# Key products that read q from SBUF instead of PSUM in the first five items of a decode kernel's second attention

## The chip, the cores and the metric

The kernel runs on one core of a Trainium2 chip. The metric is device time in microseconds (us), the median of several executions; three executions of the kernel before took 2686.34 to 2686.61 us. Beside them stands one profiled execution, whose records are read below. Its engines are named as in the profile: PE (TensorE), DVE (VectorE), ACT (ScalarE), POOL (GpSimd) and SP (SyncE, which here issues the DMA transfers). SBUF is the memory that all engines work in, PSUM the one that PE writes to; POOL's operands all lie in SBUF in this kernel.

## The reference

Two layers, each an attention block over a long cache followed by a gated feed-forward block, for one new token of a batch of two; the same weights and caches serve both layers.

```python
def _A_ref(x, k_cache, v_cache, wq, wo):           # B=2, H=32, Sk=8192, Dh=128
    q = (x @ wq).reshape(B, Sq, H, Dh).transpose(0, 2, 1, 3)
    scores = jnp.einsum("bhqd,bhkd->bhqk", q, k_cache) * (Dh ** -0.5)
    p = _softmax(scores, axis=-1)
    o = jnp.einsum("bhqk,bhkd->bhqd", p, v_cache)
    return o.transpose(0, 2, 1, 3).reshape(B, Sq, H * Dh) @ wo

x = A_x
x = x + _A_ref(_layernorm(x), A_k_cache, A_v_cache, A_wq, A_wo)
x = x + _B_ref(_layernorm(x), B_w_gate, B_w_up, B_w_down)
x = x + _A_ref(_layernorm(x), A_k_cache, A_v_cache, A_wq, A_wo)
x = x + _B_ref(_layernorm(x), B_w_gate, B_w_up, B_w_down)
```

`_B_ref` is a GEGLU block of width 4608. Everything is float32. Keys and values of one layer are 2 x 2 x 32 x 8192 x 128 x 4 bytes, 537 MB, and nearly all of that is read once for each layer.

## The kernel before

**Items.** Attention is cut into 34 items. Items 0 to 29 hold two heads of one batch row each, items 30 to 33 one head. The 8192 keys of a head are spread over the partitions: an item of two heads gives every partition 128 keys, in eight parts of 16 keys (`JC`) by 128 numbers; an item of one head has 64 keys a partition, in four parts. The first attention goes through the items from 0 to 33, the second from 33 down to 0, so that some keys and values of the last items can stay in SBUF from the first attention to the second. The first five items of the second attention are 33, 32, 31, 30 (four parts each) and 29 (eight parts); for these `waited(n)` holds and every part is worked on by itself.

**Transfers.** All large transfers are issued by SP in one fixed order, planned ahead, into places of a big SBUF tile `space`. A transfer is issued when its place has been given back by the work that last read it: keys by the sums of a part (`add_up`, L671), values by the value products on PE (L800). If that work is late, so is the issue, and all that stand behind it on SP.

**One part of keys in the first five items of the second attention** (`multiply` and `add_up`):
- PE has made q of the item on all partitions, in one of two 128-column pieces of the PSUM tile `bank` (`query`, L599), one item ahead.
- ACT copies it to SBUF, `qs[:, n % 2, :]`, once an item (L650).
- DVE multiplies the first 12 of the 16 keys of each partition by q in PSUM (L651, 1536 numbers a partition).
- POOL multiplies the other 4 keys by q in `qs` (L655, 512 numbers), and then adds the right half of the first 9 keys' products to the left half (L668, 576 numbers; both inputs in `space`).
- ACT sums up each of the last 7 keys' products (L661), and DVE reduces the folded first 9 (L671) when the next part's product has been issued.

In the first and the last part of item 33 (`at_once`) POOL folds nothing, and DVE reduces 11 keys directly. After item 33's last product `qsb` gets its second half of the q sums (L933, DVE), from which the q of later items is made. At the end of an item come the maximum (L695 to L705), the exponentials (L728, ACT) and the value products (L800, PE). In all other items DVE does the whole product and POOL all the folding; there `weigh` (L766, L771) also weights some of the values on DVE with weights that it puts in PSUM (`share`), which POOL then adds up (L774).

Each engine works through its own instructions in the order of the program; waits between engines are by semaphores. The order is written by hand (`manual_schedule`) in the loop of `attention`: product of a part, then the sums of the part before.

Of the kernel before, what the change touches and what calls it, by code (L numbers as in the profile page):

```python
# [11 lines left out]
ALU = mybir.AluOpType  # L12
# [3 lines left out]
P = 128  # L16
# [3 lines left out]
DH = 128  # L20
# [4 lines left out]
JC = 16  # L25
# [98 lines left out]
def decode_layers(ctx, tc, x_in, kc, vc, wq, wo, wg, wu, wd, out):  # L124
# [423 lines left out]
    def attention(layer):  # L548
# [37 lines left out]
        qb, S, prod, rs, mT, tot, rinv, osb = {}, {}, {}, {}, {}, {}, {}, {}  # L586
# [17 lines left out]
        def waited(n):  # L604

            return layer == 1 and n in seq[:5]

        def at_once(n, k):

            return layer == 1 and n == seq[0] and k in (0, ITEMS[n].parts - 1)  # L610
# [13 lines left out]
        def own_rows(n, k, m):  # L624

            return 11 if at_once(n, k) else 9 if waited(n) else m * JC

        def keys(n, k, m):

            key = name("k", layer, n)  # L630
            if m == 1:
                return ready[key][k]
            return part_at(arena.live[key, k][0], m * PART).rearrange("p (j d) -> p j d", d=DH)
# [3 lines left out]
        def multiply(n, k, m):  # L637

            if k == 0:
                S[n] = work.tile([P, SK * 2 // P], F32, name="S")  # L640
            u = t = keys(n, k, m)
            if n == SINGLE[1] and k == 3 and layer == 0:
                nc.scalar.copy(kept, t)
            if layer == 0 and n in KEYS_HELD:
                u = ready["products"][k % 2]
            every = m * JC
            rows = 12 if waited(n) else every
            q = qs[:, n % 2, :]
            if rows < JC and k == 0:
                nc.scalar.copy(q, qb[n])  # L650
            nc.vector.tensor_tensor(  # L651
                out=u[:, :rows, :], in0=t[:, :rows, :], in1=qb[n].unsqueeze(1).to_broadcast([P, rows, DH]), op=ALU.mult
            )
            if rows < JC:
                nc.gpsimd.tensor_tensor(  # L655
                    out=u[:, rows:, :], in0=t[:, rows:, :], in1=q.unsqueeze(1).to_broadcast([P, JC - rows, DH]),
                    op=ALU.mult,
                )
            r = own_rows(n, k, m)
            for j in range(r, every):  # L660
                nc.scalar.activation(  # L661
                    u[:, j, :], u[:, j, :], AF.Copy, accum_out=S[n][:, k * JC + j:k * JC + j + 1]
                )
            if at_once(n, k):
                prod[n, k] = u[:, :r, :]
                return
            half = prod[n, k] = u[:, :r, :DH // 2]
            nc.gpsimd.tensor_tensor(out=half, in0=half, in1=u[:, :r, DH // 2:], op=ALU.add)  # L668
# [202 lines left out]
        for i, n in enumerate(seq):  # L871
# [18 lines left out]
            if first:  # L890
                highest(p)
                softmax(p)
            for j, (k, m) in enumerate(us):
                multiply(n, k, m)
                if j == 0 and not last and not first:
                    query(seq[i + 1])
# [37 lines left out]
        n, p = seq[-1], seq[-2]  # L934
# [154 lines left out]
```

## Time and profile before

| | us |
|---|---|
| median of three executions | 2686.34 |
| the profiled execution | 2686.49 |
| its span on the core | 2684.7 |
| second attention, first five items | about 1383 to 1464 of the span |

| engine | busy, us | share of the span |
|---|---|---|
| PE | 916.5 | 34% |
| DVE | 2028.0 | 76% |
| ACT | 163.8 | 6% |
| POOL | 1551.4 | 58% |

1154.23 MB moved in the span, on average 430 GB/s. A row of the timeline reads: start in us, duration in us, engine, line of the kernel, operation, what is written<-what is read, shapes, count, and in brackets the engine's idle time before it with what ended it. Where a row stands for several instructions, the duration covers them all. A row of the windows reads: stretch, its length, then the busy time and number of instructions of each engine, PE's granted clock, the busy share of the DMA engines and GB/s. A row of SP's waits reads: who waited<-for what: us in total, times, the longest. The slices are 40 equal parts of the span, 67.1 us each.

### The profile page before, as it was taken

What the parts mean: (1) busy time and instruction counts of PE and PEld (TensorE: products, weight loads), DVE (VectorE), ACT (ScalarE), POOL (GpSimd) and SP (SyncE); (2) the same over time, 40 slices, a digit from 0 to 9 for tenths busy, and PEclk for the clock granted to TensorE, in tenths of its full rate; (3) what the DMA queues carried; (4) which work ended last, traced back from release to release, by engine and by line L of the source; (5) the groups of instructions that cost most, each with busy time, mean ns of one, the idle gap of its engine ahead of it and who ended that gap; (6) DMA issues with size and microseconds to landing.
All of it is one profiled execution on the core that took longest, in us unless ns stands there. A gap on an engine that the chain in (4) does not pass through costs nothing. (4 is left out here: it accounts for less than half of the span.)

```text
span 2684.7 us, 16125 instructions
## 1 busy us (share of the span) xinstructions
PE 916.5 (34%) x6478; PEld 290.0 (11%) x6478; DVE 2028.0 (76%) x973; ACT 163.8 (6%) x786; POOL 1551.4 (58%) x405
## 2 busy tenths in 40 slices
PE   1323332232233233334563333223323323332355
PEld 0100000000001000111221101001000100010022
DVE  4878888888888888867038878888888888888740
ACT  0000000000000000000026000000000000000000
POOL 2546676667666766744028457666766676676520
PEclk7666655665566566566986665566566556655668
DMA  9999999999999999999999999999999999999998
GB/s 422 436 436 425 437 434 434 431 432 435 433 433 432 436 431 433 435 427 426 418 413 434 433 431 436 434 432 431 435 435 431 435 432 433 433 436 429 432 424 375
DMA packets 33947, 1154.23 MB, mean 430 GB/s; under 512 B 4152, under 2 KB 4176, under 8 KB 5968
## 3 DMA queue, kind: packets, MB, share of 16 engines
q1 hardware_dynamic: 33832, 1153.19, 99.8%
q8 instruction: 51, 0.84, 0.1%
q14 instruction: 24, 0.20, 0.0%
q10 hardware_dynamic: 40, 0.01, 0.0%
HBM read 1153.18 MB, written 0.00 MB: 430 GB/s over the span
## 5 line engine op out<-in xcount | busy, mean ns | idle before, releaser
L668 POOL TENSOR_TENSOR space<-space 128x3072 f32<-128x3072 f32 (+3 forms) x221 | 1128.1, 5104 | 487.7 <-DVE space L651 349.8
L651 DVE TENSOR_TENSOR space<-space,bank 128x6144 f32<-128x6144 f32 (+3 forms) x223 | 1112.7, 4990 | 312.9 <-DMA space<-in_A_k_cache_dram 249.6
L671 DVE TENSOR_REDUCE S<-space 128x48 f32<-128x3072 f32 (+3 forms) x223 | 569.3, 2553 | 89.4 <-POOL space L668 89.1
L774 POOL TENSOR_TENSOR space<-space 128x2048 f32<-128x2048 f32 x144 | 390.1, 2709 | 385.6 <-DVE space L771 370.2
L800 PE MATMUL acc<-space,prz 128*8 128x512 f32 x3328 | 510.1, 776 | 201.7 <-DMA space<-in_A_v_cache_dram 197.7
L599 PE MATMUL bank<-qsb,pick 4*64 4x128 f32 (+1 forms) x256 | 46.3, 436 | 857.2 <-DVE space L651 847.1
L771 DVE TENSOR_TENSOR space<-space,bank 128x4096 f32<-128x4096 f32 x48 | 212.2, 4420 | 1.6
L800 PEld LDWEIGHTS acc<-space,prz 128*8 128x8 f32 x3328 | 99.6, 107 | 553.9 <-issue 345.1
L720 ACT ACTIVATE nbs<-bank 128x2 f32<-128x2 f32 (+1 forms) x68 | 11.6, 171 | 1846.2 <-PE bank L705 1799.8
L822 PE MATMUL bank<-of,osb 128*32 128x2 f32 x512 | 40.9, 202 | 237.9 <-DVE osb L815 237.9
L599 PEld LDWEIGHTS bank<-qsb,pick 4*64 4x64 f32 (+1 forms) x256 | 20.6, 200 | 878.7 <-DVE space L651 859.3
L697 PE MATMUL bank<-ident,m 128*1 128x128 f32 x68 | 21.5, 317 | 246.2 <-DVE m L695 246.1
L524 POOL TENSOR_TENSOR rstd<-ve,mhalf 128x1 f32<-128x1 f32 x4 | 2.2, 550 | 168.8 <-DVE ve L522 168.8
L779 PE MATMUL acc<-space,owner 128*8 128x512 f32 x96 | 89.9, 1039 | 0.0
L1020 DVE STREAM_TRANSPOSE o<-o 128x288 f32<-128x288 f32 x4 | 2.8, 689 | 92.4 <-ACT o L1018 92.4
L822 PEld LDWEIGHTS bank<-of,osb 128*32 128x32 f32 x512 | 35.8, 154 | 326.2 <-DVE osb L815 324.9
L736 PE MATMUL bank<-sums,unit 128*128 128x2 f32 x120 | 35.3, 363 | 87.0 <-ACT prz L728 87.0
L814 DVE TENSOR_TENSOR acc<-acc,diag 128x512 f32<-128x512 f32 x64 | 43.5, 679 | 22.9 <-PE acc L800 22.9
L841 ACT ACTIVATE oT<-bank,rinv 32x8 f32<-32x8 f32 x110 | 28.6, 260 | 381.4 <-PE bank L822 380.8
L728 ACT ACTIVATE prz<-S,nbs 64x128 f32<-64x128 f32 (+1 forms) x128 | 50.7, 396 | 17.3 <-POOL prz L718 14.4
L528 DVE TENSOR_TENSOR x<-bank,x 128x144 f32<-128x144 f32 x4 | 1.2, 308 | 65.3 <-PE bank L1046 42.6
L661 ACT ACTIVATE space<-space 128x128 f32<-128x128 f32 x164 | 48.3, 296 | 23.6 <-DVE space L651 21.5
(80 smaller groups left out, 551.5 us busy)
## 6 DMA issues: line engine op xcount, KB each, us to landing
space<-in_A_v_cache_dram SPq DMA_DIRECT2D x8, 4096.0 KB
space<-in_A_k_cache_dram SPq DMA_DIRECT2D x6, 4096.0 KB
space<-in_A_wo_dram SPq DMA_DIRECT2D x15, 1152.0 KB
space<-in_A_k_cache_dram SPq DMA_DIRECT2D x15, 1024.0 KB
space<-in_B_w_down_dram SPq DMA_DIRECT2D x9, 1152.0 KB
space<-in_B_w_gate_dram SPq DMA_DIRECT2D x3, 3456.0 KB
space<-in_A_v_cache_dram SPq DMA_DIRECT2D x10, 1024.0 KB
space<-in_A_wq_dram SPq DMA_DIRECT2D x3, 3072.0 KB
```

The costliest lines, as they stand in the source:

```text
L599: nc.tensor.matmul(qb[n][to, :], pick[32 * c:32 * c + 4, r:r + 1].to_broadcast([4, P // it.heads]), qsb[32 * c:32 * c + 4, (h % 4) * DH:(h ...
L651: nc.vector.tensor_tensor(out=u[:, :rows, :], in0=t[:, :rows, :], in1=qb[n].unsqueeze(1).to_broadcast([P, rows, DH]), op=ALU.mult)
L661: nc.scalar.activation(u[:, j, :], u[:, j, :], AF.Copy, accum_out=S[n][:, k * JC + j:k * JC + j + 1])
L668: nc.gpsimd.tensor_tensor(out=half, in0=half, in1=u[:, :r, DH // 2:], op=ALU.add)
L671: nc.vector.tensor_reduce(out=S[n][:, k * JC:k * JC + own_rows(n, k, m)], in_=prod.pop((n, k)), axis=AX.X, op=ALU.add)
L728: nc.scalar.activation(pr[at, lo:].rearrange("p (g e) -> p g e", e=4)[:, 0:it.rows // 2:2, :], s[at, :it.rows].rearrange("p (g r) -> p g r ...
L771: nc.vector.tensor_tensor(out=t, in0=t, in1=share.unsqueeze(2).to_broadcast([P, rows, DH]), op=ALU.mult)
L774: nc.gpsimd.tensor_tensor(out=t[:, :rows], in0=t[:, :rows], in1=t[:, rows:2 * rows], op=ALU.add)
L779: nc.tensor.matmul(accumulator(n)[0:8, :], owner.rearrange("p a e -> p (a e)"), part_at(arena.live[key, lo][0], 4 * DH), start=False, stop ...
L800: nc.tensor.matmul(accumulator(n)[32 * c:32 * c + 8, :], pr[:, at:at + 8], t[g // 4][:, g % 4 * 4:g % 4 * 4 + 4, :].rearrange("p j d -> p ...
L814: nc.vector.tensor_tensor(out=q, in0=q, in1=diag.unsqueeze(2).to_broadcast([P, 4, DH]), op=ALU.mult)
L822: nc.tensor.matmul(po[lo:lo + 32, i, :], t[:, i::GH], of, start=True, stop=True)
```

## The change

In `multiply`, where the product on DVE is split with POOL (only in the first five items of the second attention), all parts behind an item's first read q from the SBUF copy `qs` that POOL reads already. An item's first part, and all products elsewhere, read PSUM as before.

```diff
             q = qs[:, n % 2, :]
             if rows < JC and k == 0:
                 nc.scalar.copy(q, qb[n])
+            by = q if rows < JC and k else qb[n]
             nc.vector.tensor_tensor(
-                out=u[:, :rows, :], in0=t[:, :rows, :], in1=qb[n].unsqueeze(1).to_broadcast([P, rows, DH]), op=ALU.mult
+                out=u[:, :rows, :], in0=t[:, :rows, :], in1=by.unsqueeze(1).to_broadcast([P, rows, DH]), op=ALU.mult
             )
```

`rows` is 12 in these items and `JC` 16; `k` is the number of the part. In the built program 19 of DVE's instructions name `qs` in place of `bank`; no instruction is added or moved on any engine. Of the waits, three products (the second parts of items 33, 31 and 30) lose one for PE, and the instruction of L933 gains one.

## The prediction

> **What bounds the kernel now.** I read the page first (shares, then the slices), then the windows of the changed stretch, SP's waits in it, and the instructions in order of time.
>
> ```profile
> span 2684.7 us, 16125 instructions
> ...
> PE 916.5 (34%) x6478; PEld 290.0 (11%) x6478; DVE 2028.0 (76%) x973; ACT 163.8 (6%) x786; POOL 1551.4 (58%) x405
> ...
> DMA  9999999999999999999999999999999999999998
> GB/s 422 436 436 425 437 434 434 431 432 435 433 433 432 436 431 433 435 427 426 418 413 434 433 431 436 434 432 431 435 435 431 435 432 433 433 436 429 432 424 375
> ```
>
> No engine is full; the DMA engines are, in nearly every slice, at about 433 GB/s. The time is the bytes over that rate, and an edit to the products can only move the end if it lets the transfers run dry, or ends a time when they did. The profiled execution took 2686.49 us, 1.79 more than its span and 0.15 more than the median 2686.34; the sum is made against 2686.49.
>
> The edit touches items 33, 32, 31, 30 (one head, four parts) and 29 (two heads, eight parts). These windows are items 32, 31, 30 and 29, each from its first product on DVE to the next item's (29 to POOL's last add):
>
> ```profile
> core 0: us, PE busy (x) PEld busy (x) DVE busy (x) ACT busy (x) POOL busy (x), PEclk, DMA share, GB/s
> 1403.32:1414.48 11.16, 5.95 (x34) 1.18 (x26) 8.98 (x8) 8.72 (x57) 10.48 (x8) 0.65 1.01 418
> 1414.48:1427.65 13.17, 7.73 (x35) 2.62 (x39) 10.12 (x11) 10.81 (x61) 10.59 (x8) 0.50 1.01 420
> 1427.65:1441.56 13.91, 7.55 (x41) 2.17 (x37) 11.25 (x14) 9.15 (x60) 10.48 (x8) 0.62 1.04 439
> 1441.56:1463.66 22.10, 8.90 (x61) 2.79 (x53) 21.47 (x21) 17.94 (x115) 20.95 (x16) 0.73 1.01 433
> ```
>
> DMA stays full here too (share 1.01 to 1.04), but POOL is nearly full as well: its idle time is 0.68, 2.58, 3.43 and 1.15 us, 7.8 in all, of 60.3. And the transfers hang on this work: SP's waits between 1384 and 1470 us are
>
> ```profile
> SPq L166 <- DVE S L671: 35.6, 9, 12.8
> SPq L166 <- PE acc L800: 31.1, 8, 9.7
> ```
>
> The next cache rows are issued when the sums of a part (L671) or the value products (L800) give their place back. Compute that is late here makes issues late; what shields the time is only how far the queue is ahead.
>
> **The change part by part.** 19 of the 24 products in this stretch (three in each of items 33 to 30, seven in item 29) get q from `qs`, in SBUF, in place of `bank`, in PSUM. No instruction is added, removed or reordered.
>
> *The wait.* Item 33's second product no longer waits for PE:
>
> ```profile
> 1382.98 1.75 DVE L651 TENSOR_TENSOR space<-space,bank 128x1536 f32<-128x1536 f32 x1 [11.02 <-ACT qs L650]
> 1384.77 1.62 DVE L671 TENSOR_REDUCE S<-space 128x11 f32<-128x1408 f32 x1
> 1391.94 3.42 DVE L651 TENSOR_TENSOR space<-space,bank 128x1536 f32<-128x1536 f32 x2 [5.56 <-PE bank L599]
> ...
> 1397.82 0.75 DVE L671 TENSOR_REDUCE S<-space 128x9 f32<-128x576 f32 x1
> 1398.49 0.74 DVE L933 SCALAR_TENSOR_TENSOR qsb<-acc,rstd,qsb 128x512 f32<-128x512 f32 x1
> 1399.15 1.61 DVE L671 TENSOR_REDUCE S<-space 128x11 f32<-128x1408 f32 x1
> ```
>
> PE's q products of item 32 stood behind the wq products in PE's queue. Now the two products can start at 1386.4, 5.5 us earlier; the wait for PE passes to L933, which came 6.5 us behind it and has cover. So item 33's work alone would end 5.5 us sooner. The second parts of items 31 and 30 lose the same wait, before which DVE was not idle.
>
> *The product by itself.* 1536 elements take 1.75 us with q in PSUM; the reduce L671 takes 1.62 for 1408 elements that all come from SBUF. Both are 1.14 to 1.15 ns an element, so I price the other memory at nothing.
>
> *The price of a second SBUF stream.* This is the term that decides. Until now a product takes one tensor from SBUF and q from PSUM, and POOL works beside it undisturbed. Item 29, once it runs evenly:
>
> ```profile
> 1450.64 1.27 POOL L655 TENSOR_TENSOR space<-space,qs 128x512 f32<-128x512 f32 x1
> 1451.87 1.42 POOL L668 TENSOR_TENSOR space<-space 128x576 f32<-128x576 f32 x1
> ...
> 1461.03 1.26 POOL L655 TENSOR_TENSOR space<-space,qs 128x512 f32<-128x512 f32 x1
> ```
> ```profile
> 1452.16 1.75 DVE L651 TENSOR_TENSOR space<-space,bank 128x1536 f32<-128x1536 f32 x1
> 1453.82 0.75 DVE L671 TENSOR_REDUCE S<-space 128x9 f32<-128x576 f32 x1
> 1454.48 1.74 DVE L651 TENSOR_TENSOR space<-space,bank 128x1536 f32<-128x1536 f32 x1
> ```
>
> POOL sets the pace: (1461.03 - 1450.64) / 4 = 2.60 us a part (four parts lie between the two L655 rows), back to back, with DVE's 1.75 + 0.75 beside it. Does a DVE instruction with both tensors in SBUF also run beside POOL? The only one near POOL's work is this:
>
> ```profile
> L766 DVE TENSOR_TENSOR bank<-prz x48: 199/201/201, 212.1 to 2497.2; 128x32 f32<-128x32 f32 x48
> ...
> 1604.07 0.20 DVE L766 TENSOR_TENSOR bank<-prz 128x32 f32<-128x32 f32 x1 [0.45 <-PE bank L697]
> ...
> 1608.86 4.50 POOL L774 TENSOR_TENSOR space<-space 128x2048 f32<-128x2048 f32 x1 [7.88 <-DVE space L771]
> ```
>
> It is short and falls into POOL's 7.88 us of idle time before L774, so the trace shows no meeting of the two, and the price has two ends. Low end: products still run beside POOL, pace 2.60, nothing added. High end: product and POOL's two instructions take turns, pace 2.60 + 1.74 = 4.34. The nearest row with two SBUF tensors is POOL's own: 1.42 us for 576 elements is 2.5 ns each, over twice DVE's 1.14 with the operands in two memories. A DVE product at twice its time, 3.48 + 0.75, would set a pace of about 4.2, close to the high end by another way. I take the high end.
>
> The Trainium skill speaks for the high end: its page "SBUF — State Buffer", section "Who interferes with whom", has a DVE instruction with two SBUF inputs contend with a GpSimd instruction that reads SBUF, through a shared read interface. The page's section "A bandwidth-pool intuition that's wrong (but worth ruling out)" lets a blocked side go on about 115 ns after the other's end; with that in place of the hand-over below, the sum would be 2 us higher. No row here can confirm either.
>
> *How late the stretch ends.* In items 32 to 29 16 products are changed: 16 x 1.74 = 27.8 us, if none of them falls into POOL's idle time; 20.0 if all of that 7.8 us is used. I take it that most can't be, since it lies at the head of an item (here of item 30), where both engines wait for ACT's copy of q and then for a first product that still reads PSUM:
>
> ```profile
> 1427.70 1.27 POOL L655 TENSOR_TENSOR space<-space,qs 128x512 f32<-128x512 f32 x1 [0.99 <-ACT qs L650]
> ```
>
> Item 33 taking turns: two products to 1389.8, then POOL's four instructions (1.41, 1.27, 1.41, 1.27, about 5.2 with their overlaps) to 1395.0, the third product to 1396.7, and the 2.94 us from 1397.82 to the end of the last reduce: 1399.7 in place of 1400.8, so 1.1 us is left of the 5.5. Each turn may cost a hand-over; POOL begins 0.09 us after the product it waits for (1391.94 + 1.75 against 1393.78 in the row below), so at most 0.09 x 2 x 16 = 2.9; I take half, 1.5.
>
> ```profile
> 1393.78 1.41 POOL L668 TENSOR_TENSOR space<-space 128x576 f32<-128x576 f32 x1 [8.25 <-DVE space L651]
> ```
>
> Item 29 ends late by 24 (between 20.0 - 1.1 = 19 and 27.8 - 1.1 + 2.9 = 29.6; 24 + 1.5 with hand-overs = 25.5).
>
> *What the queue covers.* An item's keys or values are 8.39 MB (two heads x 8192 x 128 x 4 bytes), 19.4 us at 433 GB/s; a half 9.7.
>
> ```profile
> 1432.90 10.39 SPq L166 DMA_DIRECT2D space<-in_A_k_cache_dram  x2
> 1447.26 6.72 SPq L166 DMA_DIRECT2D space<-in_A_v_cache_dram  x2
> 1466.91 0.33 SPq L166 DMA_DIRECT2D space<-in_A_k_cache_dram  x1
> 1488.50 0.33 SPq L166 DMA_DIRECT2D space<-in_A_v_cache_dram  x1
> ...
> 1499.99 34.44 DMA space<-in_A_k_cache_dram
> ```
>
> The keys issued at 1499.99 land at 1534.4 (the chain that ended last), so they begin at 1515.0; the values before them at 1495.6, the keys of 1467.2 at 1476.2: that issue is 9.0 us ahead. The two halves of values before it begin at 1466.5 and 1456.8, the second half of keys (issued by 1443.3) at 1447.1, 3.8 ahead, and the DMA share stays over 1; so a transfer needs less than 3.8 us from issue to its first byte. I take 2, and 7 us of cover at 1467.2 (between 5.2 and 9). At 1443.3 only 1.8 is covered against the delay of two to three items of three changed products (5.2 us each, less 1.1: 9 to 14): the queue first runs dry there, and again after item 29. These losses don't add: what was lost at the first makes the second less early. The whole is 25.5 - 7 = 18.5 us, between 19 - 9 = 10 and 29.6 - 5.2 = 24.4. The values at 1488.5 have 6.8 us ahead, about the same. Afterwards all is shifted together and DVE, 76% busy, catches up; nothing is won back from DMA.
>
> 2686.49 + 18.5 = **2705.0 us**, with 2696.5 to 2711 as this case's own range.
>
> **Rivals.**
>
> *No contention (not slower).* The product with q in SBUF runs beside POOL as before. For it: L651 and L668 overlap in full now, and prices per element are the same. Against it: no row has DVE on two SBUF streams while POOL runs. Item 33 ends 5.5 us sooner and issues move up, but DMA is full already; at most the 418 and 420 GB/s of items 32 and 31 become 433, 3% of 24 us, 0.8 us. Time 2685.7 to 2686.5, say 2686.3. It decides if the pace of item 29 stays 2.60.
>
> *Half a wait.* DVE waits only for the POOL instruction that it finds running, and POOL never for DVE. With half an instruction, 0.67, DVE's part is 1.74 + 0.75 + 0.67 - 0.18 of overlap (1452.16 to 1454.48 is 2.32, not 2.50) = 3.0, 0.4 over POOL's pace; 16 x 0.4 = 6 less 7 of cover: nothing. With a whole one, 1.34, 3.67 a part: 16 x 1.07 = 17 - 1 - 7 = 9. So 2686 to 2696, say 2691.
>
> *The change doesn't do what it says.* The first product of each item still reads PSUM, and the wait for PE is only passed to L933. But in the program 19 products name `qs`, and L933 comes 6.5 us after the place of the old wait; if it held DVE all the same, item 33 would lose the 1.1 us again, and the forecast would be 2706.
>
> **How the numbers follow.** Taking turns 0.78, half a wait 0.10, no contention 0.10, a gain by a way that I don't see 0.02. A change below 0.2%, 5.4 us, can't be told from none in this kernel, so slower begins at 2691.7. Slower: 0.78 + 0.05 (half of the second) = 0.83; same: 0.10 + 0.05 = 0.15; faster: 0.02. The range runs from 2690, inside the second case, to 2714, 2.6 over the first's upper end of 2710.9, since the values at 1488.5 have 2.2 us less ahead than the keys; some 0.18 lies outside, 0.15 of it below.
>
> **What will show it.** Right: in item 29 the parts are 4.3 us apart in place of 2.60, as longer records of L651, L655 and L668 or as idle time before them; item 29's window ends near 1488 in place of 1463.66; the slices at 1409 to 1543 us show fewer GB/s; the 5.56 us before item 33's second product are gone; behind 1550 everything is as before, some 18 us later. Wrong: a pace of 2.6 with L651 at 1.74 beside POOL (then nothing moves), a pace near 3 (half a wait), or a late stretch with DMA still full, which would say that the queue's cover is larger than 9 us.

## The result, and the profile after

The changed kernel takes 2698.22 us (median of six executions, 2697.60 to 2699.09) against 2686.35 us (six executions, 2686.23 to 2686.74): ratio 1.0044, 95% interval 1.0031 to 1.0057, that is 11.9 us slower (8.3 to 15.3). One line was added, so that the lines behind it are one higher than before: the product is L652, POOL's product L656, its fold L669, the reduce L672.

The page of the changed kernel, its totals and the two lowest rows of the slices:

```profile
span 2695.8 us, 16124 instructions
...
PE 917.1 (34%) x6478; PEld 291.4 (11%) x6478; DVE 2034.5 (75%) x973; ACT 165.5 (6%) x786; POOL 1578.2 (59%) x405
...
DMA  9999999999999999999999999999999999999999
GB/s 420 435 435 435 433 434 432 432 434 430 435 434 430 435 432 435 433 427 425 417 411 377 416 427 433 436 431 435 435 432 433 433 434 431 435 434 429 434 424 382
```

The span grew by 11.1 us. POOL is busy 26.8 us longer and DVE 6.5, with the same instructions. Two slices, 1415 to 1550 us, fell to 377 and 416 GB/s, where they had 434 and 433. The slices behind them are as they were, within some 8 GB/s. (A tenth of 9 means 90% or more, so the DMA row hides this; GB/s does not.)

The groups of the changed kernel by shape (count | busy in us, mean ns of one | idle time before them):

```profile
L652 DVE TENSOR_TENSOR space<-space,qs 128x1536 f32<-128x1536 f32 x19 | 38.8, 2047 | 0.0
L656 POOL TENSOR_TENSOR space<-space,qs 128x512 f32<-128x512 f32 x24 | 36.5, 1524 | 14.5 <-ACT qs L650 14.5
L652 DVE TENSOR_TENSOR space<-space,bank 128x1536 f32<-128x1536 f32 x5 | 8.8, 1754 | 17.4 <-ACT qs L650 17.4
```

The five products that still read PSUM take 1.75 us as before, the 19 from SBUF 2.05 on average. The time in order shows why. First DVE, then POOL, in the steady run of item 29 of the changed kernel:

```profile
1460.71 0.76 DVE L672 TENSOR_REDUCE S<-space 128x9 f32<-128x576 f32 x1 [1.29 <-POOL space L669]
1461.38 2.13 DVE L652 TENSOR_TENSOR space<-space,qs 128x1536 f32<-128x1536 f32 x1
1464.81 0.76 DVE L672 TENSOR_REDUCE S<-space 128x9 f32<-128x576 f32 x1 [1.29 <-POOL space L669]
```
```profile
1460.64 1.26 POOL L656 TENSOR_TENSOR space<-space,qs 128x512 f32<-128x512 f32 x1
1461.86 2.91 POOL L669 TENSOR_TENSOR space<-space 128x576 f32<-128x576 f32 x1
1464.73 1.26 POOL L656 TENSOR_TENSOR space<-space,qs 128x512 f32<-128x512 f32 x1
```

At 1460.64 POOL begins its product. At 1461.38 DVE's product begins, in the records; it takes 2.13, its own 1.74 and 0.39 more, which is what was left of L656 (to 1461.90) within 0.13. At 1461.86 the fold begins and takes 2.91, its own 1.41 and 1.50 more: it ends 1.26 behind the end of DVE's product (1463.51), so it did nearly all of its work after that. The blocked side's waiting stands inside its record, not as idle time before it. The reduce L672, with one input in SBUF, runs beside L656 at its usual 0.75. The pace is 1464.81 - 1460.71 = 4.10 us a part in place of 2.60.

Items 32, 31, 30 and 29 of the changed kernel in windows (length, busy time and number for each engine, clock, DMA share, GB/s):

```profile
1400.62:1416.22 15.60, 5.15 (x34) 1.07 (x26) 9.86 (x9) 8.99 (x57) 14.91 (x8) 0.72 1.02 422
1416.22:1431.90 15.68, 8.82 (x39) 2.64 (x39) 11.29 (x12) 11.13 (x61) 14.98 (x8) 0.54 1.01 408
1431.90:1447.58 15.68, 7.66 (x37) 2.34 (x41) 12.75 (x13) 9.49 (x60) 14.98 (x8) 0.57 0.87 352
1447.58:1479.64 32.06, 8.40 (x57) 2.79 (x49) 24.01 (x21) 18.61 (x115) 31.50 (x16) 0.66 0.97 409
```

Against the same items before they are 4.4, 2.5, 1.8 and 10.0 us longer, 18.7 together. POOL's busy time (the fifth) grew by 23.9, and its idle time fell from 7.8 to 2.65. Item 32 starts 2.7 us earlier than before (1400.62 against 1403.32), so item 29 ends 16.0 us late. DMA loses less than that: three stretches of the changed kernel,

```profile
1430.00:1440.00 10.00, 2.82 (x16) 1.00 (x9) 7.56 (x7) 6.63 (x43) 9.30 (x6) 0.67 0.82 304
1470.00:1490.00 20.00, 1.65 (x7) 0.87 (x7) 15.06 (x9) 5.99 (x37) 16.47 (x8) 0.50 0.83 344
1500.00:1510.00 10.00, 4.52 (x44) 1.79 (x36) 9.97 (x5) 0.00 (x0) 5.42 (x2) 0.95 0.80 315
```

hold most of the missing bytes: (433 - 304) / 433 x 10 + (433 - 344) / 433 x 20 + (433 - 315) / 433 x 10 = 9.8 us of the 11.1. In each of them DMA picks up when SP issues again. In steps of 2 us it moves 82 GB/s at 1436 to 1438, until the half key issue of 1437.67 (1432.90 before); it moves nothing at 1480 to 1482 and at 1502 to 1504, until the first two of these issues:

```profile
1482.90 0.33 SPq L166 DMA_DIRECT2D space<-in_A_k_cache_dram  x1
1504.57 0.33 SPq L166 DMA_DIRECT2D space<-in_A_v_cache_dram  x1
1515.97 0.33 SPq L166 DMA_DIRECT2D space<-in_A_k_cache_dram  x1
```

These three issues stood at 1466.91, 1488.50 and 1499.99 before: each is 16.0 to 16.1 us later, as late as item 29's end.

### The profile page after: what moved, and what is told of

Same layout as the page of the kernel before. It is cut to its first block, busy times and chain, and to the rows that moved or that the text cites. A ratio compares the mean times of both kernels' runs of the same rounds, so it can differ in the third digit from the quotient of the medians.

```text
span 2695.8 us, 16124 instructions
## 1 busy us (share of the span) xinstructions
PE 917.1 (34%) x6478; PEld 291.4 (11%) x6478; DVE 2034.5 (75%) x973; ACT 165.5 (6%) x786; POOL 1578.2 (59%) x405
## 5 line engine op out<-in xcount | busy, mean ns | idle before, releaser
L669 POOL TENSOR_TENSOR space<-space 128x3072 f32<-128x3072 f32 (+3 forms) x221 | 1148.8, 5198 | 474.1 <-DVE space L652 337.7
L652 DVE TENSOR_TENSOR space<-space,bank 128x6144 f32<-128x6144 f32 (+3 forms) x204 | 1079.8, 5293 | 301.8 <-DMA space<-in_A_k_cache_dram 244.7
L672 DVE TENSOR_REDUCE S<-space 128x48 f32<-128x3072 f32 (+3 forms) x223 | 569.4, 2553 | 104.2 <-POOL space L669 104.0
L698 PE MATMUL bank<-ident,m 128*1 128x128 f32 x68 | 21.7, 319 | 247.0 <-DVE m L696 246.9
```

The costliest lines, as they stand in the source:

```text
L652: nc.vector.tensor_tensor(out=u[:, :rows, :], in0=t[:, :rows, :], in1=by.unsqueeze(1).to_broadcast([P, rows, DH]), op=ALU.mult)
L672: nc.vector.tensor_reduce(out=S[n][:, k * JC:k * JC + own_rows(n, k, m)], in_=prod.pop((n, k)), axis=AX.X, op=ALU.add)
```

## The experiments

Theory: a DVE product with both inputs in SBUF and those of POOL's instructions that read SBUF take turns; the stretch ends late, and the end moves by what the queue of transfers doesn't cover. "Lateness" below is the start of item 28's first product in the profiled execution of each kernel, less 1461.77 us, where it starts before. Times are medians, the difference is to the kernel before on the same chip, intervals are of the ratio.

| kernel | lateness, us | time added, us | ratio, 95% interval | lateness less time added |
|---|---|---|---|---|
| item 33's second and third part only | -4.2 | -0.2 | 0.9991 to 1.0009 | - |
| filler of 3 x 128, q in PSUM | 5.0 | 1.5 | 0.9994 to 1.0014 | 3.5 |
| items 33 to 30 only | 6.1 | 3.9 | 1.0006 to 1.0024 | 2.2 |
| item 29 only | 9.8 | 5.8 | 1.0013 to 1.0031 | 4.0 |
| filler of 6 x 128, q in PSUM | 10.5 | 6.2 | 1.0015 to 1.0033 | 4.3 |
| POOL writes only | 11.0 | 7.4 | one execution | 3.6 |
| the changed kernel | 16.0 | 11.9 | 1.0031 to 1.0057 | 4.1 |
| DVE with its own copy of q | 16.4 | 13.2 | 1.0037 to 1.0062 | 3.2 |
| all 24 products | 20.6 | 17.0 | 1.0050 to 1.0077 | 3.6 |
| filler of 13 x 128, q in PSUM | 25.0 | 21.4 | 1.0067 to 1.0094 | 3.6 |

The lateness comes from one execution of each kernel, the time added from medians, and the executions of one kernel spread over up to 2.6 us (the filler of 3 x 128). Against the time of the very execution that was profiled, the last column runs from 2.1 to 4.9.

**Half the change each.** Which items cost the time?

```diff
-            by = q if rows < JC and k else qb[n]
+            by = q if n == PAIRS - 1 and rows < JC and k else qb[n]
```

> q from SBUF only in item 29 (seven products). Turn-taking between DVE's product and POOL's two instructions: seven L652 records of about 2.1 us, L669 of 2.9, 4.1 us a part in item 29, the items before it as in the kernel before; item 29 ends 10 us late (that is what the changed kernel's item 29 lost by itself), the queue covers about 5 of them at the values issued after it, so +5 us, 2691.5. Rival, the loss comes from the earlier start of item 33 and the order of issues that follows: no loss, 2686.3. Rival, each of the 19 products costs the same share of the 12 us: 7/19 of 12, +4.4.

```diff
-            by = q if rows < JC and k else qb[n]
+            by = q if n >= PAIRS and rows < JC and k else qb[n]
```

> q from SBUF only in items 33 to 30 (twelve products). Turn-taking with a cover at each issue: item 29 starts 6 us late as in the changed kernel and runs at 2.6 us a part, so the queue runs dry only at the two half key transfers around 1438 and 1449 us, where the changed kernel's landings were 3.2 and 4.8 us late: +4.8 us, 2691, and no dry stretch behind item 29. If the cover of 5 us behind item 29 were all that counts: 6 - 5, +1. If each product costs the same: 12/19 of 12, +7.6.

Measured 2692.23 us (+5.8) for item 29 alone and 2690.35 (+3.9) for the others. In the first, five of the seven products take 2.13 or 2.14 us and the item ends 9.8 us late, with nothing late before it; so the loss doesn't need item 33's earlier start. The first run doesn't exclude an equal share for each product (+4.4 is in its interval, +3.5 to +8.3), the second does: +7.6 lies outside +1.6 to +6.4. By its median the second also loses more than one cover of 4 or 5 us behind item 29 would let it (6.1 - 4 = 2.1 at most), though its interval reaches that far down. Its profile shows the loss where the half key transfers stand, before item 29 is done: 306 GB/s at 1430 to 1440 us, and 444 at 1470 to 1490.

**The wait alone.** Item 33's later products are freed from PE, and only one of POOL's folds meets a product.

```diff
-            by = q if rows < JC and k else qb[n]
+            by = q if n == seq[0] and rows < JC and k in (1, 2) else qb[n]
```

> q from SBUF only in item 33's second and third part; the wait for PE is gone there and POOL is idle at the first of the two. Turn-taking: one L669 meets the second product and is 1.5 us longer, no product is; item 33 ends a little earlier or as before and DMA is full, so no change, 2686.3 within 1 us. Rival, the earlier start is worth time by itself: faster by up to 0.8 us. Rival, reading q from SBUF is slow for DVE by itself: two products longer than 1.75 us.

Measured 2686.30 us against 2686.47. DVE, then POOL, of this kernel:

```profile
1386.05 3.42 DVE L652 TENSOR_TENSOR space<-space,qs 128x1536 f32<-128x1536 f32 x2
...
1391.91 1.75 DVE L652 TENSOR_TENSOR space<-space,bank 128x1536 f32<-128x1536 f32 x1 [0.39 <-PE bank L599]
```
```profile
1387.88 2.85 POOL L669 TENSOR_TENSOR space<-space 128x576 f32<-128x576 f32 x1 [2.60 <-DVE space L652]
...
1391.92 1.41 POOL L669 TENSOR_TENSOR space<-space 128x576 f32<-128x576 f32 x1
```

One kernel has both cases. The second of the two products from SBUF ran while the fold wanted to, and the fold took 2.85; the third product, from PSUM, began within 0.01 us of the next fold, and both took their usual 1.75 and 1.41. The two from SBUF take 3.42 together, as they did from PSUM: by itself the other memory costs nothing. The items behind run 4.2 us earlier than before, and the time is the same (interval within 2.4 us either way): no gain from earlier compute shows where DMA is full.

**Another address.** Do the two collide on `qs`, which both read?

```diff
                 nc.scalar.copy(q, qb[n])
+                if n != seq[0]:
+                    nc.scalar.copy(xt[:, PAD + n % 2 * DH:PAD + n % 2 * DH + DH], qb[n])
-            by = q if rows < JC and k else qb[n]
+            own = xt[:, PAD + n % 2 * DH:PAD + n % 2 * DH + DH]
+            by = (q if n == seq[0] else own) if rows < JC and k else qb[n]
```

> Behind item 33, DVE reads q from a second SBUF copy in another tile (xt), which POOL does not read; ACT makes it, 16 products changed. Turn-taking over a shared way into SBUF, whatever the addresses: L652 (here L655) 2.1, L669 (L672) 2.9, 4.1 us a part, time as the changed kernel, 2698, up to 1 us more for ACT's second copy at the head of an item. Rival, the two engines collide on the same tile qs: products 1.75, POOL 1.41 and 1.27, pace 2.6, time 2686 to 2687.

Measured 2699.63 us. DVE, then POOL, of this kernel (lines three higher than in the changed kernel):

```profile
1461.82 2.14 DVE L655 TENSOR_TENSOR space<-space,xt 128x1536 f32<-128x1536 f32 x1
```
```profile
1462.31 2.91 POOL L672 TENSOR_TENSOR space<-space 128x576 f32<-128x576 f32 x1
```

The same 2.14 and 2.91 with different tiles for q, so they don't collide on `qs`. They don't collide on `space` either: both read it in the kernel before, without turns. That what they share is a way into SBUF is argued from this, and the kernel with memsets below bears it out. The time is 1.4 us above the changed kernel's, where up to 1 was expected; the value issue of 1488.50 comes 17.4 us late here, 16.1 in the changed kernel.

**More of it.** The first part of each item reads `qs` too.

```diff
-            by = q if rows < JC and k else qb[n]
+            by = q if rows < JC else qb[n]
```

> All 24 products read q from SBUF, the first part of each item too. Turn-taking: the first product of each item now meets POOL's L655 that starts in the same moment, one more turn of 1.3 to 1.7 us in each of five items, so item 29 ends 16 + 5 to 8 us late; +16 to 20 us, 2702 to 2706. Rival, what costs is only the steady run of parts where POOL is never idle: the first parts add nothing, 2698. First products may also start without waiting for PE, which is ACT's wait anyway.

Measured 2703.48 us (+17.0), lateness 20.6. POOL, item 29 of this kernel, its first two products of q:

```profile
1451.31 2.84 POOL L656 TENSOR_TENSOR space<-space,qs 128x512 f32<-128x512 f32 x1 [0.17 <-ACT qs L650]
...
1455.47 2.79 POOL L656 TENSOR_TENSOR space<-space,qs 128x512 f32<-128x512 f32 x1
```

The L656 that starts with the first product now takes 2.84 in place of 1.28. That product began at 1451.27, 0.04 us before it. So turns are also taken at the head of an item. They add 4.6 us of lateness in five items, a little less than the 5 to 8 expected.

**Lateness without turns.** q stays in PSUM, and DVE gets other work, a filler whose results go into a small tile `spare` that nothing reads. Against the kernel before, with 13 x 128 numbers (`spare` is made further up); the other two kernels have 6 and 3 in place of 13:

```diff
+            if rows < JC and k and n != seq[0]:
+                nc.vector.tensor_reduce(
+                    out=spare[:, :13], in_=same.unsqueeze(1).to_broadcast([P, 13, P]), axis=AX.X, op=ALU.add
+                )
             nc.vector.tensor_tensor(
```

> q from PSUM as in the kernel before, and ahead of each of the 16 later products in items 32 to 29 an extra reduce on DVE (13 x 128 numbers, one SBUF input, about 1.9 us), so that the pace is 1.74 + 0.75 + 1.9 less overlaps, 4.1 us a part, with no two-input product. The extra work adds nothing to the result. If lateness against the queue's cover is all that costs: L651 1.75, POOL 1.27 and 1.41, item 29 ends 16 to 19 us late, queue dry at the same places, +11 to 14 us, 2697 to 2701. Rival, the taking of turns costs DMA or PE something of its own: clearly less than +11, down to 2686.

> As the run with 13, but 6 x 128 numbers, about 0.95 us: pace 3.2 us a part, 0.6 over the kernel before. 16 x 0.6 = 9.6 less what falls into POOL's and DVE's idle time: item 29 ends 4 to 7 us late, near the cover of 5 behind it and above the cover at the two half key transfers: 0 to +3 us, 2686 to 2689.5. If there were no cover: +4 to 7.

> As the runs with fillers, with 3 x 128 numbers, about 0.55 us before each of the 16 products: pace 2.8 us a part against POOL's 2.6. By the line that the runs so far lie on (time added = lateness of item 28's first product less about 4 us), a lateness of 3 to 6 us gives 0 to +2 us, 2686 to 2688.5. If there were no cover, +3 to 6.

Measured 2707.89, 2692.64 and 2687.88 us (+21.4, +6.2, +1.5). The first two are outside what was expected, because the items became later than expected: 25.0 and 10.5 us in place of 16 to 19 and 4 to 7. The filler costs DVE its full length also at places where turn-taking cost POOL less: with 13 x 128, items 32, 31 and 30 lose 4.6, 3.8 and 4.4 us (4.4, 2.5 and 1.8 in the changed kernel), and item 29 12.5, since its first two steps from product to product take 5.1 and 4.6 us before the pace settles at the expected 4.1 to 4.2. The relation holds all the same. The +6.2 of the second alone would fit "no cover" (+4 to 7); it is the 10.5 us of lateness beside it that show a cover. The +1.5 of the third is not clear of nothing (interval -1.6 to +3.8). DVE, then POOL, with 13 x 128:

```profile
1482.69 1.88 DVE L653 TENSOR_REDUCE spare<-same 128x13 f32<-128x1664 f32 x1
1484.48 1.75 DVE L656 TENSOR_TENSOR space<-space,bank 128x1536 f32<-128x1536 f32 x1
```
```profile
1482.19 1.41 POOL L673 TENSOR_TENSOR space<-space 128x576 f32<-128x576 f32 x1 [1.49 <-DVE space L656]
1483.55 1.27 POOL L660 TENSOR_TENSOR space<-space,qs 128x512 f32<-128x512 f32 x1
```

No record is stretched here, and the time added is again the lateness less 3.5 to 4.3. So turn-taking has no second price for DMA or PE that shows within about 1 us; being late is what it costs.

**A POOL that only writes.**

```diff
             if rows < JC:
+                if k:
+                    for _ in range(4):
+                        nc.gpsimd.memset(u[:, rows:, :], 0.0)
+                else:
                     nc.gpsimd.tensor_tensor(
                     ...
```

> As the changed kernel, but in the 19 later parts POOL writes zeros four times into the last four keys' products in place of multiplying them by q (the scores of these keys are left out there). POOL's memsets only write; its fold L669 still reads. If only reading instructions of POOL take turns with a two-input product: a product that begins beside memsets takes 1.75 us, and only folds that meet a product grow, to 2.9. If any POOL instruction with an address in SBUF takes turns: products beside memsets grow by the rest of the memset, up to 0.5 us. No expectation for the time beyond 2686 to 2700.

The one execution took 2693.83 us. DVE, then POOL, in item 29 of this kernel:

```profile
1451.24 2.54 DVE L652 TENSOR_TENSOR space<-space,qs 128x1536 f32<-128x1536 f32 x1
...
1465.36 1.75 DVE L652 TENSOR_TENSOR space<-space,qs 128x1536 f32<-128x1536 f32 x1
```
```profile
1450.76 1.40 POOL L673 TENSOR_TENSOR space<-space 128x576 f32<-128x576 f32 x1
1452.10 2.27 POOL L658 MEMSET space<- 128x512 f32 x4
...
1464.60 2.27 POOL L658 MEMSET space<- 128x512 f32 x4
1466.84 1.53 POOL L673 TENSOR_TENSOR space<-space 128x576 f32<-128x576 f32 x1
```

The product at 1465.36 runs beside memsets from 1464.60 to 1466.87 and takes 1.75; all groups of four memsets in this item take 2.26 to 2.28. So do two that have no product beside them, in items 33 and 32 (2.27 from 1394.55, 2.26 from 1412.69). The product at 1451.24 meets a fold that ends at 1452.16: 2.54 is 1.74 and 0.80, within 0.12 of the rest of that fold. POOL's products and folds, which read SBUF, take turns with DVE's product; its memsets, which only write, do not.

No version beats the kernel before: the only part of the change that makes compute earlier, the wait in item 33, brings nothing that shows.

## Why the prediction was right

*The direction and the mechanism.* The forecast case, taking turns, is what the traces show: pace 4.10 where 4.34 was worked out, against 2.60 for "no contention" and 3.0 to 3.67 for "half a wait". That rival falls by the fold's record: POOL waits for DVE too, 1.50 us each time. The third rival falls as well: all 19 products read `qs`, and L934 (L933 before) did not hold DVE.

This is also where the Trainium skill was right. Its page "SBUF — State Buffer", section "Who interferes with whom", has a DVE instruction with two SBUF inputs contend with a GpSimd instruction that reads SBUF, and not with one that only writes it. This case's traces agree: 2.91 us of fold beside such a product, 1.41 beside one from PSUM, and 1.75 of product beside memsets. The 115 ns of the Trainium skill's page, section "A bandwidth-pool intuition that's wrong (but worth ruling out)", were measured there on a DMA whose descriptors GpSimd writes, held up by a DVE copy. The prediction charged them to both sides of two tensor instructions, which is more than the page says. They did not show here: the fold ended 1.26 us behind the product, less than its own 1.41.

*The price of the product by itself* was put at nothing, rightly: two take 3.42 us with POOL idle at the first, shown in the kernel with the wait alone. The prediction's second way to the high end, a product at twice its time, is not what happens: in the steady run it takes 2.13 us, and 1.75 beside an idle POOL. That this way gave 4.2, nearer to the 4.10 measured than 4.34 is, was chance.

*The lateness of item 29 was mis-sized*: 25.5 us in the sum, 16.0 measured. Four parts make the difference. A turn costs 1.49 us, not 1.74 (POOL's busy time grew by 23.9 / 16), since DVE's record and POOL's overlap at their ends: 3.9. POOL's idle time took up 5.2 of its 7.8 us, not the 2.7 that was left in the sum: 2.5. The argument that most of it lies at the heads of items and can't be used was wrong twice. Part of it lies elsewhere: in item 30 POOL of the kernel before waited for DVE's last product (row below), and in the changed kernel that time is used. And of the waits at the heads, the 0.99 and 0.93 us before items 30 and 29 fell to 0.18 and 0.17, because POOL came to them later. What can't be used is 2.65 us.

```profile
1439.27 1.41 POOL L668 TENSOR_TENSOR space<-space 128x576 f32<-128x576 f32 x1 [1.98 <-DVE space L651]
```

There is no hand-over: 1.5. In item 33 the third product ran from 1391.69 to 1393.83, between L656 and the second fold, and not behind all of POOL's four instructions, which left 2.7 us of the earlier start and not 1.1: 1.6. Together 9.5.

*The cover was mis-sized too*, the other way: 7 us in the sum, 4.1 measured (4.9 against the profiled execution). The issue that decides is not the key issue of 1466.91 but the value issue of 1488.50, which the prediction gave 6.8 us ahead; less the 2 that it took for the start of a transfer, that is 4.8. The prediction called the two about the same, but it compared 6.8 before that subtraction with 7 behind it, so the larger cover went into the sum.

The kernels bear this out. Take how late each of them makes the value issue of 1488.50, less 4.8, and compare it with what its profiled execution took over 2686.49:

| kernel | value issue late, us | less 4.8 | profiled execution, added us |
|---|---|---|---|
| item 29 only | 9.9 | 5.1 | 5.0 |
| filler of 6 x 128 | 11.1 | 6.3 | 6.3 |
| POOL writes only | 12.1 | 7.3 | 7.3 |
| the changed kernel | 16.1 | 11.3 | 11.1 |
| DVE with its own copy of q | 17.4 | 12.6 | 12.8 |
| all 24 products | 21.2 | 16.4 | 16.2 |
| filler of 13 x 128 | 26.5 | 21.7 | 22.4 |

Read at the issue that waits, and within one execution, the cover of the first six is 4.6 to 5.0 us, and 4.0 for the last.

*The half key transfers.* The loss there is real (304 GB/s at 1430 to 1440) and, as forecast, does not add to the later one. The two halves of the change lose 5.8 and 3.9 us, and both together 11.9. That is the 16.0 us of lateness less one cover, as if the early loss had not been. The delay at that place was put too high: 9 to 14 us, where the issue of 1442.96 came at 1448.43, 5.5 late. In the kernel with items 33 to 30 alone it came at 1448.18; 5.2 late less the prediction's cover of 1.8 is 3.4, near the 3.9 measured, while the value issue, 7.4 late, would give 2.6.

So the sum added 18.5 us and the measurement 11.9: 9.5 too much lateness less 2.9 too much cover is the 6.6 between them. That the two errors work against each other is luck. The time lies inside the range and, with 2698.2, inside the case's own range of 2696.5 to 2711.

*What is not settled*: the 2 us for the start of a transfer was a choice below 3.8, and no run measures it by itself. The filler of 3 x 128 doesn't fit the working above: its value issue is 5.0 us late, which leaves 0.2, and its profiled execution, the slowest of ten, took 2.9 more (1.5 by the median, within noise of nothing).

## What to carry to other kernels

Before moving an operand from PSUM to SBUF to spare a wait, count the SBUF inputs of the DVE instruction: here the second one made it take turns with both of POOL's instructions that read SBUF (1.5 us of POOL's time for each product of 1.74). In a kernel that is bound by transfers, translate lateness into time by the queue's lead at the issue that waits for the late work, and look for the issue whose delay exceeds its lead by most, not for the first one. Such waiting hid inside the records of both engines here, so compare a record's duration with the same shape elsewhere before looking for idle time.

## What the runs showed of the hardware

Beside a DVE product with two SBUF inputs, POOL's fold of 1.41 us grows to 2.85 to 2.93 (once to 3.03), and its product of 1.27 to 2.77 to 2.92. DVE's product grows from 1.75 to at most 2.49 in the changed kernel, and to 2.82 in the kernel with memsets. Which side waits is mostly decided by whose record begins first, but not when the two begin almost together. In the changed kernel POOL's record begins 0.05 us before DVE's, and it is POOL that waits:

```profile
1450.78 2.91 POOL L656 TENSOR_TENSOR space<-space,qs 128x512 f32<-128x512 f32 x1
```
```profile
1450.83 1.74 DVE L652 TENSOR_TENSOR space<-space,qs 128x1536 f32<-128x1536 f32 x1
```

A product with q in PSUM that begins 0.01 us before a fold leaves it at 1.41. POOL's memsets run beside the product from SBUF at 2.26 to 2.28 us for four, as they do without it.
